# Warm-up matmuls of 256 columns in place of twice as many of 128, and the first Q turned ahead of the first K piece

## The chip, the cores and the metric

The kernel runs on one core of one Trainium2 chip. The metric is the time of one execution on the device in microseconds (us); lower is better. A core has a matrix engine (PE, whose weight loads are listed as PEld), a vector engine (DVE), an activation engine (ACT), GpSimd (POOL) and a sync engine (SP) that here issues most DMAs. Each engine takes its instructions strictly in the order in which they were put down for it; between engines they wait on semaphores.

## The reference, cut to what matters

Attention whose queries are averaged in pairs, followed by a max-out MLP. Batch 8, 8 heads, sequence 1152, head size 64; after the pairing there are 576 queries a head.

```
q_pool = q.reshape(B, H, S // 2, 2, D).mean(axis=3)
scores = 1/sqrt(D) * q_pool @ k^T
attn   = softmax(scores)
x      = (attn @ v), heads side by side       # 4608 x 512
g      = maximum(x @ w1, x @ w2)              # 4608 x 1024
out    = g @ w_out                            # 4608 x 512, float32
```

All inputs are float32; the kernel works in bfloat16 with float32 accumulation. The ones that the changed matmuls multiply are no part of this: their products are never read.

## The kernel before, in words

Two heads form a pair; there are 32 pairs. For each pair K, Q and V are loaded, cast to bfloat16 (Q: its two rows added, which is the pairing), and K and Q are transposed so that the head size lies on the partitions. Scores come in groups of 512 columns for both heads (`scores`, L302, four or more matmuls into two PSUM banks); one ACT instruction a group takes the exponential (`exps`, L317, a tile of 128x1024). Later matmuls multiply by V (L621, L636), DVE normalizes, and the MLP's matmuls (L760, L803, L846) are woven between.

The order of everything is written out by hand in one long string. Each character is a step: `S` the scores of the next group on PE, `E` its exponential on ACT, `K` and `Q` the transposes of the next piece of K and of Q on PE, `g` and `b` the copies of their results from PSUM to SBUF on DVE, `f` a cast of K on ACT, `k` a cast of K on POOL, `y` the add of Q's rows on DVE, `l` and `u` the next load on SP and on ACT, `F` a fill job. A character puts one step at the end of its own engine's queue, so the string fixes only the order within each engine; steps of different engines are ordered by their data. A second string, `BANKS`, gives the PSUM bank of each PE step in the order of opening.

The first pair comes in pieces so that work can start early. K arrives in four pieces (tiles 0-2, 2-4, 4-6, 6-9); the first two are cast on ACT (L418), the last two on POOL (L424). Each is transposed by PE (`ktrans_pe` with `halves`, L552) and copied to kT by DVE (L568). Q arrives in two pieces (units 0-4 and 4-9, L358 loads); DVE adds the rows (L428, `cast_q0`), PE transposes (`qtrans`, L533), DVE copies to qpT (L540). The first scores need the first piece of both.

Ahead of this PE multiplies ones with ones ("fill"). DVE writes ones into 128 columns of the tile `rem` (L399); PE runs 28 matmuls of 128x128 on them into bank 7 and two fill jobs of two matmuls each (L515); 14 more fill jobs (28 matmuls) stand singly in the string among the first groups of scores. In all there are 60 such matmuls, each with its weight load.

The start of the order string before is `luFFlulllfyKQklgfbSkKEFlgFKSgESyFFlKEFgQSbE`. On PE it reads: fills, K piece 0, Q piece 0, scores 0, K piece 1, F, F, K piece 2, scores 1, scores 2, F, F, K piece 3, F, Q piece 1, scores 3. On DVE: ones, add Q piece 0, copy K piece 0, copy Q piece 0, copy K pieces 1 and 2, add Q piece 1, copy K piece 3, copy Q piece 1.

## Time and profile before

| what | us |
|---|---|
| median of 3 runs | 358.02 |
| lowest and highest of them | 357.6 and 358.13 |
| span of the profiled execution, first to last instruction | 356.4 |
| PE busy | 346.0 (97%) |
| ACT busy | 313.8 (88%) |
| DVE busy | 230.1 (65%) |
| POOL busy | 151.4 (42%) |

The profiled execution's own time is its span; the run's time also holds what lies around the first and the last instruction. In the profile a line such as `L515` is the line of the kernel that recorded the instruction. A group's busy time counts the stretch in which at least one of its instructions is in flight. PE's matmuls overlap, so the durations of single matmuls are longer than the distance from one start to the next. The chain lists the work that ended last, followed back from the end; what is not on it was finished early enough.

### The profile page before, as it was taken

Reading aid. Unit: us, or ns where it says so; the run is one execution under the profiler, and the core shown is the slowest. Engines: PE = TensorE matmul, PEld = TensorE weight load, DVE = VectorE, ACT = ScalarE, POOL = GpSimd, SP = SyncE. Lnnn points to the kernel's source line nnn. Section 1 sums busy time; section 2 is a strip of 40 time slices with the busy share of each in tenths; the row PEclk is TensorE's granted clock in tenths of the full one; section 3 lists DMA queues with packets and bytes.
Section 4 is the critical chain, followed back from the end, with each engine's and each line's share of the span. In section 5 each row is a group of like instructions: output and inputs, shape, how many; then the busy total and the mean of one; then the engine's idle time right before and its main releaser. Section 6 shows DMA issues by size and latency. Waiting matters only on the chain.

```text
span 356.4 us, 13757 instructions
## 1 busy us (share of the span) xinstructions
PE 346.0 (97%) x6178; PEld 218.5 (61%) x6178; DVE 230.1 (65%) x472; ACT 313.8 (88%) x354; POOL 151.4 (42%) x136
## 2 busy tenths in 40 slices
PE   7889999999899999999999999999999999999996
PEld 5556665656564675656666576556576757448753
DVE  2587589974966867985887677785586875414001
ACT  5999999999999899999999989989999796992431
POOL 2625997554564264355544455227444621010000
PEclk9999999999999999999999999999999999999999
DMA  8999999999989989998999699998999943012215
GB/s 271 403 397 398 370 255 309 280 289 261 293 252 279 315 196 350 237 301 183 278 320 260 153 230 301 237 314 234 224 299 255 267 68 75 17 32 47 61 31 148
DMA packets 76699, 84.55 MB, mean 237 GB/s; under 512 B 48480, under 2 KB 49760, under 8 KB 76640
## 3 DMA queue, kind: packets, MB, share of 16 engines
q1 hardware_dynamic: 75856, 83.15, 87.5%
q8 instruction: 48, 0.79, 0.9%
q10 hardware_dynamic: 784, 0.52, 0.5%
q14 instruction: 11, 0.09, 0.1%
HBM read 62.91 MB, written 9.44 MB: 203 GB/s over the span
## 4 chain that ended last, share of the span: by engine, by line
PE 87%; ACT 9%; DMA 2%; issue 1%; SPq 0%; DVE 0%
PE ps L803 25%; PE ps L621 20%; PE ps L302 19%; PE ps L760 16%; ACT et L317 9%; PE ps L636 3%; PE ps L593 2%; DMA qraw<-in_q_dram 2%; PE ps L846 1%; PE ps L552 0%; PE ps L533 0%; SPq L346 0%; DVE qp L428 0%; SPq L358 0%; PE ps L730 0%
## 5 line engine op out<-in xcount | busy, mean ns | idle before, releaser
L317 ACT ACTIVATE et<-ps 128x1024 bf16<-128x1024 f32 (+1 forms) x336 | 302.4, 1019 | 14.5 <-PE ps L302 9.7
L302 PE MATMUL ps<-qpT,kT 64*128 64x256 bf16 (+7 forms) x1162 | 117.3, 283 | 2.7 <-issue 1.1
L485 DVE STREAM_TRANSPOSE qpT<-qp 32x288 bf16<-32x288 bf16 x216 | 101.4, 469 | 10.4 <-PE ps L302 6.1
L760 PE MATMUL ps<-xT,wd 64*128 64x512 bf16 (+3 forms) x832 | 81.2, 311 | 0.2
L302 PEld LDWEIGHTS ps<-qpT,kT 64*128 64x128 bf16 x1162 | 48.3, 94 | 49.7 <-ACT et L317 11.3
L803 PE MATMUL ps<-wo,stage 64*128 64x512 bf16 x544 | 76.4, 376 | 0.0
L435 POOL TENSOR_TENSOR qp<-qraw 128x576 bf16<-128x576 f32 x30 | 42.1, 1406 | 61.1 <-DMA qraw<-in_q_dram 57.3
L621 PEld LDWEIGHTS ps<-vE,et 128*128 128x128 bf16 x1728 | 54.9, 97 | 13.9 <-ACT et L317 9.3
L621 PE MATMUL ps<-vE,et 128*128 128x65 bf16 x1728 | 60.7, 193 | 0.7 <-issue 0.3
L771 DVE TENSOR_SCALAR stage<-ps 128x1024 bf16<-128x1024 f32 (+3 forms) x41 | 39.7, 970 | 21.1 <-PE ps L760 20.6
L760 PEld LDWEIGHTS ps<-xT,wd 64*128 64x128 bf16 x832 | 35.6, 94 | 22.2 <-PE ps L760 1.9
L405 POOL TENSOR_SCALAR kbf<-kraw 128x1152 bf16<-128x1152 f32 x31 | 35.7, 1153 | 26.3 <-DMA kraw<-in_k_dram 25.6
L803 PE MATMUL ps<-w,xT 64*128 64x512 bf16 x272 | 40.8, 377 | 0.0
L803 PEld LDWEIGHTS ps<-wo,stage 64*128 64x128 bf16 x544 | 26.4, 94 | 20.5
L445 POOL TENSOR_SCALAR vE<-vraw 128x1152 bf16<-128x1152 f32 x24 | 27.4, 1154 | 19.4 <-PE ps L636 10.8
L809 DVE COPY stage<-ps 128x1024 f32<-128x1024 f32 x14 | 17.1, 1224 | 23.1 <-PE ps L803 23.0
L468 POOL TENSOR_SCALAR stage<-et 128x1152 bf16<-128x1152 bf16 x14 | 16.1, 1152 | 35.5 <-ACT et L317 35.5
L654 DVE TENSOR_TENSOR xnat<-ps,rc 128x256 bf16<-128x256 f32 (+2 forms) x71 | 27.6, 397 | 2.0
L651 DVE RECIPROCAL rc<-ps 128x4 f32<-128x4 f32 (+2 forms) x64 | 11.6, 182 | 25.9 <-PE ps L621 25.5
L621 PEld LDWEIGHTS ps<-stage,et 128*128 128x128 bf16 x576 | 18.1, 97 | 2.7 <-issue 2.6
L621 PE MATMUL ps<-stage,et 128*128 128x65 bf16 x576 | 19.7, 193 | 0.0
L803 PEld LDWEIGHTS ps<-w,xT 64*128 64x128 bf16 x272 | 12.5, 94 | 8.8 <-DVE stage L771 0.2
(55 smaller groups left out, 155.4 us busy)
## 6 DMA issues: line engine op xcount, KB each, us to landing
vraw<-in_v_dram SPq DMA_DIRECT2D x32, 576.0 KB, 6.1
kraw<-in_k_dram SPq DMA_DIRECT2D x31, 576.0 KB, 6.7
qraw<-in_q_dram SPq DMA_DIRECT2D x31, 576.0 KB, 6.3
out_dram<-stage SPq DMA_DIRECT2D x24, 256.0 KB, 4.1
out_dram<-stage SPq DMA_DIRECT2D x21, 128.0 KB, 3.4
xT<-in_moe_w_dram SPq DMA_DIRECT2D x4, 512.0 KB, 12.2
stage<-in_moe_w_out_dram SPq DMA_DIRECT2D x4, 512.0 KB, 14.1
stage<-in_moe_w_dram SPq DMA_DIRECT2D x4, 512.0 KB, 13.2
```

What stands on the lines that cost most here:

```text
L302: last = e.matmul(ps[:, h, col:col + hi - lo], kT[i % 3][rows(h), t, :], qpT[i % 3][rows(h), lo:hi], start=True, stop=True)
L317: op("ACT", lambda e: e.activation(et2[:, :, c:c + z - a], ps[:, :, a - g * W:z - g * W], EXP, scale=scale), r=[f"b{m}", f"b{m + 1}"], w=w ...
L405: op("POOL", lambda g: g.tensor_scalar(kbf[s][:, :, :, :].rearrange("p t h d -> p h t d"), kraw[r][:, :, :, :], 1.0, 1.0, ALU.mult, ALU.mu ...
L435: op("POOL", lambda g: g.tensor_tensor(qpf[s][:, :, :], qraw[r][:, :, 0, :], qraw[r][:, :, 1, :], ALU.add), r=[f"qraw{r}"], w=[f"qp{s}.0", ...
L445: return g.tensor_scalar(vE[r][:, :, :, 0:D].rearrange("p t h d -> p h t d"), vraw[s][:, :, :, :], 1.0, 1.0, ALU.mult, ALU.mult)
L485: op("DVE", lambda e: e.transpose(view[dst:dst + 32, :, 32 * pb:32 * pb + 32], qpf[s][src:src + 32, :, 32 * db:32 * db + 32]), r=[f"qp{s}. ...
L621: last = e.matmul(fb[m][:, at * 66:at * 66 + 65], et[:, a:a + P], vE[vs][:, t, half, 0:65], start=(t == 0), stop=(t == NT - 1))
L654: todo.append(evac_op("DVE", lambda e, m, z=z, at=at, num=num, dst=dst: e.tensor_tensor(dst, a(m)[z, at:at + num, 0:D], rc[k][z, at:at + n ...
L760: last = e.matmul(fb[m + k][:, 0:size], wd[z, ct, (f0 + k) * P:(f0 + k + 1) * P], xT[z, ct, n0:n1], start=(turn == 0 and ct == 0), stop=(t ...
L771: return e.tensor_scalar_max(gT[:, f0:f0 + 2, g0:g0 + size], wide[m // 2][:, :, 0:size], 0.0)
L803: last = e.matmul(fb[m + k][:, :], lhs, rhs, start=(turn == 0 and j == 0), stop=(turn == 1 and j == NC_ + NF - 1))
L809: return e.tensor_copy(osb2[:, o:o + 2, :], wide[m // 2][:, :, :])
```

## The change

The ones cover 256 columns instead of 128, and each fill matmul multiplies 128 of them by all 256; 14 instead of 28 stand at the start, and one instead of two in each fill job. The total of columns streamed by fills stays as it is; the matmuls on ones fall from 60 to 30, with as many weight loads. In the order string `KQ` becomes `QK` and the copy `b` goes ahead of the copy `g`, so on PE the first Q piece is transposed ahead of the first K piece and on DVE it is copied first. The bank string is turned to match, so each step keeps its bank. Costs named in the code (`cost=`) are not used by it.

```
-    FILL = 28
+    FILL = 14
...
-        "0124605424023623462032424660232342630240624702402064202420472042646264246024604640164604264126402406"
+        "0142605424023623462032424660232342630240624702402064202420472042646264246024604640164604264126402406"
...
-                op("DVE", lambda e: e.memset(rem[:, 0, :, :], 1.0), w=["rem0"], cost=0.1)
-                op("PE", lambda e: fill(e, 7, FILL), r=["rem0"], w=["b7"], cost=0.0563 * FILL, mode="f",
+                op("DVE", lambda e: e.memset(rem[:, 0:2, :, :], 1.0), w=["rem0"], cost=0.15)
+                op("PE", lambda e: fill(e, 7, FILL), r=["rem0"], w=["b7"], cost=0.1126 * FILL, mode="f",
...
-            one = rem[:, 0, :, :].rearrange("p h c -> p (h c)")
+            one = rem[:, 0:2, :, :].rearrange("p t h c -> p (t h c)")
             for _ in range(n):
-                last = e.matmul(fb[m][:, 0:P], one, one, start=True, stop=True)
+                last = e.matmul(fb[m][:, 0:2 * P], one[:, 0:P], one, start=True, stop=True)
             return last
...
-            return Job(("f", n), 1, [(["rem0"], 0.0563 * 2, "f", False, lambda e, m: fill(e, m, 2))], [])
+            return Job(("f", n), 1, [(["rem0"], 0.1126, "f", False, lambda e, m: fill(e, m, 1))], [])
...
-            "luFFlulllfyKQklgfbSkKEFlgFKSgESyFFlKEFgQSbESlFkSFEFFKlEySFSgESlqFFEFQlSbEFkSQElbKvSEgSlESceAAEATcESA"
+            "luFFlulllfyQKklbfgSkKEFlgFKSgESyFFlKEFgQSbESlFkSFEFFKlEySFSgESlqFFEFQlSbEFkSQElbKvSEgSlESceAAEATcESA"
```

## The prediction

> **What bounds the kernel now.** I read the page's totals first, then the chain in order of time, because the change lies wholly in the first 14 us and only the chain tells what an early microsecond is worth.

> ```profile
> span 356.4 us, 13757 instructions
> ...
> PE 346.0 (97%) x6178; PEld 218.5 (61%) x6178; DVE 230.1 (65%) x472; ACT 313.8 (88%) x354; POOL 151.4 (42%) x136
> ```

> PE is the busy engine over the whole span, but the start looks different. The chain, first rows:

> ```profile
> 2.24 5.91 DMA qraw<-in_q_dram
> 8.15 0.02 issue
> 8.17 0.50 DVE qp L428
> 8.67 0.04 issue
> 8.72 0.34 PE ps L533 x10
> 9.06 0.34 PE ps L302 x4
> 9.40 0.02 issue
> 9.43 15.70 ACT et L317 x17
> 25.12 0.04 issue
> 25.17 0.41 PE ps L552 x16
> ```

> Until 8.15 us the end of the kernel hangs on one transfer, the second piece of the first Q. From it a short line of single steps (add, transposes, scores) leads to the fourth exponential at 9.43, and from there 17 exponentials follow without a gap until 25.12. Only then does PE take the chain. So whatever the change does ahead of 9.43 counts only if it moves that transfer, that line of steps, or the feeding of ACT between 9.43 and 25.12.

> The start in single steps, from the timeline, all engines together in order of time:

> ```profile
> 0.90 0.17 DVE L399 MEMSET rem<- 128x128 bf16 x1 [0.90 <-PEq L1027]
> ...
> 1.12 3.41 PE L515 MATMUL ps<-rem 128*128 128x128 bf16 x32 [1.12 <-DVE rem L399]
> ...
> 3.92 0.43 DVE L428 TENSOR_TENSOR qp<-qraw 128x256 bf16<-128x256 f32 x1 [2.85 <-DMA qraw<-in_q_dram]
> ...
> 4.31 0.86 ACT L418 ACTIVATE kbf<-kraw 128x256 bf16<-128x256 f32 x2 [1.20 <-DMA kraw<-in_k_dram]
> ...
> 4.78 0.23 PE L552 MATMUL ps<-ident,kbf 64*128 64x64 bf16 x4 [0.25 <-ACT kbf L418]
> ...
> 4.95 0.31 PE L533 MATMUL ps<-ident,qp 64*64 64x64 bf16 x8
> 5.06 0.29 DVE L568 COPY kT<-ps 128x256 bf16<-128x256 bf16 x1 [0.71 <-PE ps L552]
> 5.22 1.03 POOL L424 TENSOR_SCALAR kbf<-kraw 128x256 bf16<-128x256 f32 x2 [3.65 <-DMA kraw<-in_k_dram]
> 5.30 0.29 DVE L540 COPY qpT<-ps 128x256 bf16<-128x256 bf16 x1
> ...
> 5.65 0.39 PE L302 MATMUL ps<-qpT,kT 64*128 64x256 bf16 x4 [0.39 <-DVE qpT L540]
> ```

> The first Q piece is ready at 3.92 + 0.43 = 4.35, the first K piece at 4.31 + 0.86/2 = 4.74, and PE is done with the fills at about the time the Q is ready. As K stands first, Q waits 0.6 us for it (4.95 instead of 4.35), and the first scores wait for the copy of Q, the last of the four steps.

> ACT in this stretch:

> ```profile
> 6.08 2.85 ACT L317 ACTIVATE et<-ps 128x1024 bf16<-128x1024 f32 x3 [0.91 <-PE ps L552]
> 9.43 2.85 ACT L317 ACTIVATE et<-ps 128x1024 bf16<-128x1024 f32 x3 [0.49 <-PE ps L302]
> ```

> Three exponentials end at 8.93, then ACT idles 0.49 us for the line of steps that the transfer holds. This idle is the cover of everything that is gained or lost ahead of it.

> **The change part by part.** *Q ahead of K.* A hand-over from DVE to PE takes 0.06 (the copy of Q ends at 5.59, scores start at 5.65), from PE to DVE 0.04 to 0.05 (transposes end at 5.01, copy at 5.06). Q's 8 transposes then start at 4.35 + 0.06 = 4.41 and end at 4.72; their copy runs from 4.77 to 5.06. K's start stays at 4.78, bound by the cast, since Q's instructions have long been issued; its copy starts at 5.06 as before, ends at 5.35, and the scores start at 5.41 instead of 5.65: 0.24 us earlier. What follows on PE and DVE moves with it: K piece 1 has been cast by 4.31 + 0.86 = 5.17, piece 2 by 5.22 + 1.03/2 = 5.74, before they are asked for. So the three exponentials run from 5.84 to 8.69. The fourth does not move: its scores stand behind the second Q's transposes on PE, and the copy of K piece 3 stands behind the second Q's add on DVE, and both wait for the landing at 8.15. What is late next is thus that transfer, and the idle time of 0.49 becomes 0.73. Gain on the end: 0. Its bounds are 0 and, if that transfer were free by then, -0.24.

> The moved step brings 8 transposes on PE and one copy on DVE, no DMA. On PE it passes K's four transposes, on DVE K's copy; SP, ACT and POOL keep their queues word for word, so no transfer is issued earlier or later. It adds one thing: PE now waits for Q's add ahead of K's cast. Behind that wait stand K, the scores and all later PE work. In this trace Q is ready 0.39 us before K; Q would have to come later than that to hold K back, and the scores need both anyhow.

> *Ones of 256 columns.* The memset takes 0.17 for 128 columns. The wider one is not in the trace; the nearest rows are DVE's copies of several widths and its widest slow form:

> ```profile
> L568 DVE COPY kT<-ps 128x256 bf16<-128x256 bf16 x3 | 0.9, 292 | 1.5 <-PE ps L552 1.5
> L540 DVE COPY qpT<-ps 128x576 bf16<-128x576 bf16 x4 | 1.8, 458 | 2.8 <-PE ps L533 2.8
> L498 DVE TENSOR_REDUCE wo<-stage 128x1024 bf16<-128x1024 f32 x4 | 4.8, 1210 | 0.0
> ```

> The copies give (458 - 292)/320 = 0.52 ns a column, 0.07 us for 128 more; the slow form 1.2 ns, 0.15 us; nothing at all is the other end. I take 0.07, as a memset is nearer to a copy. Fills start at 1.19.

> *Half as many fills.* Their pace shows the clock better than the clock column does:

> ```profile
> 3.00:3.50 0.50, 0.50 (x8) 0.50 (x6) 0.00 (x0) 0.11 (x1) 0.00 (x0) 1.00 1.05 325
> ```

> ```profile
> 1.73 2.80 PE L515 MATMUL ps<-rem 128*128 128x128 bf16 x26
> ```

> ```profile
> 3.97 0.56 PE L515 MATMUL ps<-rem 128*128 128x128 bf16 x5
> ```

> ```profile
> 10.36 0.51 PE L515 MATMUL ps<-rem 128*128 128x128 bf16 x6
> ...
> 11.51 0.29 PE L515 MATMUL ps<-rem 128*128 128x128 bf16 x2
> ```

> From 1.73 to 3.97 there are 26 - 5 = 21 steps in 2.24 us, 0.107 each; late fills step (0.51 - 0.29)/4 = 0.055. So PE runs at half speed up to about 4.2 us, although the window prints a clock of 1.00 (it has no record for that time), and at full speed after. A fill of 128 columns is paced by its columns in both states, with its weight load beside it, so one of 256 should cost what two cost now: 0.213 slow, 0.11 fast. The 16 at the start then end as before to within the memset's 0.07, about 4.42 instead of 4.37, which is when Q comes ready: no cost. The 14 single jobs stream the same columns; each drops one weight load that was hidden anyway. They all lie between 6.03 and 13.9, where the chain is a transfer, the line of steps (no fill in it), or ACT: 0 on the end. If the cover were gone, 14 times the difference between two small and one large would count, by these rows under 0.01 us each, 0.1 in all.

> [...]

> *Sum:* 0 on the span of 356.4 (bounds -0.24 and +0.1). The runs' median lies 358.02 - 356.4 = 1.6 above the span, around which nothing changes. Forecast 358.0 us.

> **The rivals.**
> *The clock opens later or closes again (slower).* The fills are there in effect to hold the clock. It opened 4.2 - 1.12 = 3.1 us after the first fill. If what opens it counts instructions or weight loads rather than columns, half as many may not do it, and PE is at half speed when the line at 8.72 runs; that is the point from which it decides. Price: the line's ten transposes stream 5 pairs of 64 columns and its scores 2 pairs of 256, at 128 columns in 0.053 about 0.13 + 0.21 = 0.34 us, which doubles: +0.34. Then, per exponential of 0.95 us (2.85/3), PE's scores alone grow from 0.21 to 0.43, and with fills (0.11 a job) and 18 transposes of 64 columns in pairs (0.24) the load goes from some 0.6 to 1.2, over the 0.95 that ACT takes: 0.2 to 0.3 lost at each of three exponentials. Together about +1.0, 359.0. Against it: a fill leaves PE as busy with 256 columns as with two times 128, and in the trace the clock held through the gap from 8.1 to 8.7.

> [...]

> *PE's instruction stream is lighter (faster).* The source view of the fill line has a row for time in which PE stood before a fill for no shown reason:

> ```profile
>   issue: 0.8, 4
> ```

> Four times 0.2 us. If PE's own queue handling is what these are, 30 fewer matmuls and weight loads give back up to 0.8 us, and if ACT between 9.43 and 25.12 is in truth fed late by PE, the end moves by as much: 357.2. Against it: the chain shows no gap in ACT there, so I see no way for it to reach the end. [...]

> *It does not bring Q forward.* If the fills ran over (the memset at +0.15 and the opening late), Q would start up to 0.3 later and the first scores stay at 5.65. The fourth exponential would still be at 9.43: 358.0, no difference.

> **How the numbers follow.** A measurement of this kernel can tell about 0.2% from no change, 0.7 us. Forecast (0 on the end) 0.44; Q not brought forward, also no change, 0.08; clock 0.28; lighter stream 0.20. So faster 0.20, same 0.52, slower 0.28. The clock has more than the lighter stream because it has a path to the end, and the other needs one that the chain doesn't show. The no-change cases alone would span 357.6 to 358.3 (the runs' spread and the bounds). The range must leave out no more than 2 in 10: it takes in 357.2 and 359.0 with 0.3 around them, 356.9 to 359.3.

> **What would show it.** Right: fills in 16 steps of 0.213 to about 4.2, then 0.11; Q's transposes ahead of K's at 4.4; first scores near 5.4; three exponentials ending near 8.7; the idle before the fourth grown to about 0.7; the fourth at 9.4 and 17 without a gap. Wrong: matmuls after 4.5 us still at half pace (clock rival); the second Q's add not at 8.2; gaps in ACT between 9.4 and 25; or a difference that first appears after 25 us, where the change touches nothing.

## The result: slower, and the profile after

The changed kernel takes 361.33 us (median of 22 runs, 358.57 to 366.32), the kernel before 358.43 in the same 22 rounds (357.02 to 360.69). The ratio is 1.0067, with a 95% interval of 1.0046 to 1.0088: 0.67% or 2.4 us slower. The ratio leaves out the two of the 22 runs that lie more than 1.5% above the fastest (364.89 and 366.32), so it is a little below that of the medians, which differ by 2.9 us. The forecast was no change, 358.0, in a range that ended at 359.3. The profiled execution has a span of 361.8 us against 356.4: it loses 5.4 us, more than the medians differ.

The start did what it should. Rows of the changed kernel's timeline, PE and DVE in the first 9 us, then ACT:

```profile
0.93 0.27 DVE L399 MEMSET rem<- 128x256 bf16 x1 [0.93 <-PEq L1027]
...
1.26 3.33 PE L515 MATMUL ps<-rem 128*128 128x256 bf16 x16 [1.26 <-DVE rem L399]
...
4.52 0.31 PE L533 MATMUL ps<-ident,qp 64*64 64x64 bf16 x8
...
4.76 0.23 PE L552 MATMUL ps<-ident,kbf 64*128 64x64 bf16 x4
...
5.42 0.39 PE L302 MATMUL ps<-qpT,kT 64*128 64x256 bf16 x4 [0.42 <-DVE kT L568]
...
7.27 0.49 DVE L428 TENSOR_TENSOR qp<-qraw 128x320 bf16<-128x320 f32 x1 [0.58 <-DMA qraw<-in_q_dram]
```

```profile
5.85 19.42 ACT L317 ACTIVATE et<-ps 128x1024 bf16<-128x1024 f32 x22 [0.68 <-PE ps L552]
25.46 4.69 ACT L317 ACTIVATE et<-ps 128x1024 bf16<-128x1024 f32 x5 [0.19 <-PE ps L302]
```

Q goes ahead of K, the first scores start at 5.42, and the clock opens at 4.18 by the trace's clock record (4.20 before). In this execution the second Q piece also came in early enough (its add starts at 7.27 instead of 8.17), so 22 exponentials run with no gap from 5.85: the fourth is 0.85 us earlier than before.

The time is lost later. I paired the exponentials of the two traces by their number and took the lag of the changed kernel, that is, how much later each starts than before: -0.85 us at the fourth, +0.17 at 31 us, +0.8 at 131, +1.3 at 182, and then one jump from +1.3 to +4.4 at 285 us and to +5.3 at 292. The waits of PE between 100 and 300 us, in the view of who waited for whom, first before, then after (us in total, times, longest):

```profile
PEld ps L621 <- issue: 2.8, 13, 0.2
```

```profile
PEld ps L621 <- issue: 6.4, 17, 2.5
PE ps L621 <- issue: 2.9, 2, 2.4
```

"Issue" is idle time for which the profile knows no releaser. Before, it comes in portions of 0.2 us ahead of the weight loads; after, matmuls multiplying by V stand still for 2.4 us at a stretch. The place on PE's timeline, first before, then after:

```profile
281.95 2.35 PE L621 MATMUL ps<-stage,et 128*128 128x65 bf16 x72
```

```profile
283.23 1.93 PE L621 MATMUL ps<-stage,et 128*128 128x65 bf16 x58
287.54 0.93 PE L621 MATMUL ps<-stage,et 128*128 128x65 bf16 x14 [2.38 <-issue]
```

The same 72 matmuls, without any wait written between them, run through before, and after they are cut into 58 and 14. And the stall costs more than itself. The windows view of the changed kernel around it (columns: busy time of PE, PEld, DVE, ACT, POOL, then granted clock, DMA share and GB/s):

```profile
285.00:287.50 2.50, 0.16 (x6) 0.06 (x3) 0.76 (x2) 0.06 (x1) 2.50 (x3) 1.00 1.10 99
287.50:289.00 1.50, 1.46 (x20) 1.09 (x21) 0.46 (x3) 0.00 (x0) 0.55 (x1) 0.50 0.88 344
289.00:291.00 2.00, 2.00 (x18) 0.92 (x14) 0.52 (x2) 1.94 (x2) 1.15 (x1) 0.53 0.31 68
```

After the idle time the clock is at half from 287.48 to 290.90 by the clock record, 3.41 us. The lag grows by 4.1 us in all (from +1.3 to +5.4): 2.4 are the stall, and the other 1.7 are half of the 3.41 us at half clock. In three of the 22 runs the mean clock is 0.995 as here; they are the three slowest, 363.5 to 366.3. The other 19 have a median of 360.82, still 2.4 us above 358.43, so the halved clock makes single runs worse but the loss does not need it.

What PE lacked there, as the rest of this document argues, were instructions. The page of the profile lists a DMA queue that carries them:

```profile
q8 instruction: 48, 0.79, 1.0%
```

48 packets with 0.79 MB are blocks of 16 KB. PE has 6148 matmuls, as many weight loads and some 60 waits, about 12,400 instructions; 0.79 MB over these is 64 bytes each, and by that estimate a block holds 256 of them, 128 pairs of weight load and matmul less the waits. I counted the matmuls in both traces up to each stall without a releaser, and set the time at which a block's transfer ended beside the time at which PE went on. A stall is given from the start of the matmul ahead of it to the start of the one behind it, so it is some 0.2 to 0.35 us longer than the idle time:

| kernel | stall on PE, us | matmul it stands before | block transfer, us | from its end to PE, us |
|---|---|---|---|---|
| before | 28.49 to 29.04 | 474 | 26.54 to 27.64 | 1.40 |
| before | 91.22 to 92.70 | 1620 | 90.30 to 91.40 | 1.30 |
| after | 28.89 to 30.12 | 474 | 27.57 to 28.70 | 1.42 |
| after | 130.03 to 130.76 | 2258 | 127.90 to 129.24 | 1.52 |
| after | 284.96 to 287.54 | 5062 | 285.14 to 286.20 | 1.34 |

The matmuls 1620, 2258 and 5062 are 9, 14 and 36 times 127.4 behind 474, though these are different steps of the program in the two kernels: the stalls lie at block borders, and each ends 1.3 to 1.5 us after a transfer. The eleven traces of the experiments below bear this out: over all thirteen there are 28 idle stretches of 0.3 us or more on PE without a releaser, and every one stands before matmul 474 or 1, 9, 10, 14, 36 or 37 blocks of 127.4 behind it. That a block is asked for when PE begins the one ahead of it is my reading, as no trace records the asking. Counted from there, up to 4.7 us pass until its transfer starts (before and after), about 2 us in the median from 95 to 290 us (2.1 before, 2.3 after); behind 290 us, where the page of the changed kernel has 19 to 62 GB/s on the DMA queues up to 353 us (101 to 403 ahead of that), it is 1.1 us at most. So a block of short matmuls was used up before the next one had come. In the place above the block ahead of the border holds some 63 matmuls at 17 ns and 58 at 32 ns in the changed kernel, and PE needs 3.4 us for it; the next block's transfer started 3.6 us after PE had begun it. Before, a border lies in the same run of 72, after 28 of them; the block ahead of it holds fewer short matmuls and takes 4.3 us, the transfer started after 0.8 us, and PE does not stall. The change takes 30 pairs out of the start, and with that moves all later borders by 30 matmuls.

That gives a reckoning that can be tested. For each block I took the time that PE needs for it at the pace of before, and the shortage against a need of delay + 1.1 (transfer) + 1.4 us, averaged over the delays seen in the two traces. This is an estimate, made after the result was known. Summed: 3.2 us with the borders of before, 5.6 with 30 pairs fewer, 4.6 with 16 fewer, 4.3 with 64 more, 5.6 with 98 more (98 is 128 - 30), 3.2 again with 128 more.

### The profile page after: what moved, and what is told of

The parts are those of the page before. It is cut to its first block, busy times and chain, and to the rows that moved or that the text cites. A ratio compares the mean times of both kernels' runs of the same rounds, so it can differ in the third digit from the quotient of the medians.

```text
span 361.8 us, 13697 instructions
## 1 busy us (share of the span) xinstructions
PE 348.6 (96%) x6148; PEld 217.6 (60%) x6148; DVE 230.3 (64%) x472; ACT 314.1 (87%) x354; POOL 151.3 (42%) x136
## 4 chain that ended last, share of the span: by engine, by line
PE 75%; ACT 15%; DMA 6%; issue 2%; DVE 1%; POOL 0%; SPq 0%
PE ps L803 21%; PE ps L621 17%; PE ps L302 16%; ACT et L317 15%; PE ps L760 14%; DMA xT<-in_moe_w_dram 4%; PE ps L636 2%; DMA qraw<-in_q_dram 2%; PE ps L593 2%; PE ps L846 1%; PE ps L515 1%; POOL qp L435 0%; PE ps L552 0%; DVE xT L498 0%; DVE stage L809 0%
## 5 line engine op out<-in xcount | busy, mean ns | idle before, releaser
L317 ACT ACTIVATE et<-ps 128x1024 bf16<-128x1024 f32 (+1 forms) x336 | 302.6, 1021 | 19.5 <-PE ps L302 14.5
L302 PE MATMUL ps<-qpT,kT 64*128 64x256 bf16 (+7 forms) x1162 | 118.0, 284 | 2.6 <-DVE kT L568 0.7
L760 PE MATMUL ps<-xT,wd 64*128 64x512 bf16 (+3 forms) x832 | 82.1, 314 | 0.2
L302 PEld LDWEIGHTS ps<-qpT,kT 64*128 64x128 bf16 x1162 | 48.3, 94 | 50.5 <-ACT et L317 11.3
L803 PE MATMUL ps<-wo,stage 64*128 64x512 bf16 x544 | 76.4, 376 | 0.0
L405 POOL TENSOR_SCALAR kbf<-kraw 128x1152 bf16<-128x1152 f32 x31 | 35.6, 1151 | 22.4 <-DMA kraw<-in_k_dram 20.6
L803 PE MATMUL ps<-w,xT 64*128 64x512 bf16 x272 | 40.8, 377 | 0.0
L803 PEld LDWEIGHTS ps<-wo,stage 64*128 64x128 bf16 x544 | 26.4, 94 | 20.5
L803 PEld LDWEIGHTS ps<-w,xT 64*128 64x128 bf16 x272 | 12.5, 94 | 8.9 <-DVE stage L771 0.2
```

The lines of the kernel that those rows point to most:

```text
L302: last = e.matmul(ps[:, h, col:col + hi - lo], kT[i % 3][rows(h), t, :], qpT[i % 3][rows(h), lo:hi], start=True, stop=True)
L317: op("ACT", lambda e: e.activation(et2[:, :, c:c + z - a], ps[:, :, a - g * W:z - g * W], EXP, scale=scale), r=[f"b{m}", f"b{m + 1}"], w=w ...
L405: op("POOL", lambda g: g.tensor_scalar(kbf[s][:, :, :, :].rearrange("p t h d -> p h t d"), kraw[r][:, :, :, :], 1.0, 1.0, ALU.mult, ALU.mu ...
L760: last = e.matmul(fb[m + k][:, 0:size], wd[z, ct, (f0 + k) * P:(f0 + k + 1) * P], xT[z, ct, n0:n1], start=(turn == 0 and ct == 0), stop=(t ...
L803: last = e.matmul(fb[m + k][:, :], lhs, rhs, start=(turn == 0 and j == 0), stop=(turn == 1 and j == NC_ + NF - 1))
```

## Experiments

All ratios are to the kernel before, run in the same rounds, with 95% intervals. Theory 1 is the one above; theory 2 says that the earlier start shifts the later transfers.

**The two halves apart.** Fills alone (the changed kernel with order and banks of before; cut):

```
-            "luFFlulllfyQKklbfgSk...    BANKS "0142605424...
+            "luFFlulllfyKQklgfbSk...    BANKS "0124605424...
```

> The 256-column fills alone; K stays ahead of Q. Theory 1 (instruction supply): PE's instructions arrive in blocks of 16 KB, 48 of them in the trace; the stalls without a releaser in both traces lie at matmuls 474, 1620, 2258 and 5062, which are 9, 22 and 27 times 127.4 apart from the first, and each ends 1.3 to 1.5 us after a 16 KB instruction transfer ended. 30 matmuls and their weight loads fewer move the block borders by 30 matmuls, into the dense runs of attention-times-V matmuls, where a block is used up in 3.4 us instead of 4.4 to 4.8. Worked out from the pace of the trace before and the delays of the instruction transfers in both traces: 5.6 us of such stalls in a run instead of 3.2, so +2.3 us here, ratio about 1.0065, the whole change. Theory 2 (earlier start): the first scores come 0.24 us earlier and all later transfers fall otherwise; then this kernel, whose first scores come no earlier, is like the one before, ratio 1.000.

The expectation miscounts the distances: they are 9, 14 and 36 blocks from the first. Measured: 362.18 us (6 runs), 1.0106 (1.0066 to 1.0145). Q first alone, the opposite edit (fills of before, order and banks of the change):

> Q ahead of K alone; 60 fills of 128 columns as before. Theory 1: the count of PE's instructions is that of before and so are the block borders; ratio 1.000 to 0.999 (the first scores 0.24 us earlier). Theory 2: the whole change, ratio about 1.0065.

Measured: 358.03 us, 1.000 (0.9978 to 1.0021). The fills alone make the whole loss, Q first neither costs nor gains: theory 2 is out, since here the first scores start earlier without a loss, and the fills alone lose without them (5.79). PE's timeline of the fills-alone kernel shows the cut at the same place, 14 matmuls from the end:

```profile
283.81 1.67 PE L621 MATMUL ps<-stage,et 128*128 128x65 bf16 x50
286.05 0.58 PE L621 MATMUL ps<-stage,et 128*128 128x65 bf16 x14 [0.56 <-issue]
```

(The view begins at 284 us; the run of matmuls began at 283.56 and has 58.) Here PE is idle for only 0.56 us: the block's transfer started 1.7 us after it was asked for, against 3.6 in the changed kernel.

**The count restored.**

```
-                op("PE", lambda e: fill(e, 7, FILL), ...      # 14 of 256 columns
+                op("PE", lambda e: pad(e, 7, 44), ...         # 44 of 81 columns
```

> The changed kernel with its first 14 fills cut into 44 of 81 columns: 60 matmuls on ones as before, Q first, all later fills with 256 columns. Theory 1: 30 more matmuls than the changed kernel, and faster by 2.3 us for it: ratio to before 1.000. Theory 2 and a third one, that the 256 columns themselves cost (the clock, the memset): like the changed kernel, about 1.0065.

Measured: 358.72 us, 1.0005 (0.9984 to 1.0025). More matmuls, and the loss is gone, with the wide ones, the memset and the order of Q as in the change. In its timeline the 72 matmuls are whole again:

```profile
282.94 2.43 PE L627 MATMUL ps<-stage,et 128*128 128x65 bf16 x72
```

This execution also bears on the clock rival. Its clock opened only at 13.32 us, ACT had to wait for scores, and the fourth exponential started at 10.43, 1.0 us later than before; at the end the lag is 1.1 us, close to the price that the prediction put on a late clock. But this is the kernel without the loss, and in the changed kernel's trace, which loses 5.4 us, the clock opened at 4.18.

**Half the dose.**

```
-                op("DVE", lambda e: e.memset(rem[:, 0, :, :], 1.0), ...
+                op("DVE", lambda e: e.memset(rem[:, 0:2, :, :], 1.0), ...
...
-            [(["rem0"], 0.0563 * 2, "f", False, lambda e, m: fill(e, m, 2))]
+            [(["rem0"], 0.1126, "f", False, lambda e, m: wide_fill(e, m, 1))]   # 1 of 256; first 28 of 128 kept
```

> Before, with only the 16 fill jobs made of one matmul of 256 columns; the 28 first fills have 128. 16 matmuls and weight loads fewer. Theory 1 by the same reckoning: 4.6 us of stalls instead of 3.2, +1.4 us, ratio 1.004, between before and the change. Theory 2: 1.000.

Measured: 359.58 us, 1.0031 (1.0014 to 1.0049). The place of the cut moves with the count:

```profile
283.81 1.34 PE L627 MATMUL ps<-stage,et 128*128 128x65 bf16 x39
286.57 1.00 PE L627 MATMUL ps<-stage,et 128*128 128x65 bf16 x28 [1.42 <-issue]
```

(Of the 44 matmuls ahead of the cut the view, which begins at 284 us, holds 39.) The cut stands 28 matmuls from the end instead of 14: with 16 pairs fewer the border falls 14 matmuls earlier in the program than with 30 fewer.

**Adding late.** Two kernels add work on PE well behind the start of the changed kernel, ahead of the first matmul of L803 in the program, which then overwrites it:

```
+                    if n == 0 and j == 0 and turn == 0:
+                        for _ in range(30):
+                            e.matmul(fb[m][0:32, 0:16], ident[:, 0:32], ident[:, 0:16], start=True, stop=True)
```

> The changed kernel with 30 small matmuls (32x16, with their weight loads) added on PE ahead of the first p job, at about matmul 1890, near 113 us; their products are overwritten. Theory 1 (instruction supply): from there on the block borders are those of before again, and the blocks at matmuls 2131, 3533 and 4934 stall some 2.5 us less in sum by the reckoning (1.4 each instead of 0.5, 0.4 and 0.7); the added work costs 30 times about 0.03, 0.8 to 0.9 us. So added work makes it faster than the changed kernel by about 1.6 us: ratio to before about 1.002. Rival (the loss is made in the first 14 us, by the clock or the early transfers, and added work only costs): 1.009.

```
+                        for _ in range(4):
+                            e.matmul(fb[m][:, :], ident[:, :], w21[:, 0, :], start=True, stop=True)
```

> The changed kernel with 4 matmuls of 512 columns at the same place instead: about the same PE time (4 times 0.216, 0.86 us), but only 4 instead of 30 more instructions of each kind. Theory 1: the borders move by 4 and the stalls stay, so it is slower than the changed kernel by what it adds: ratio to before about 1.009. Rival: like the 30 small ones, whatever they give.

Both expectations place the added work wrongly: in the traces it runs at 69.4 to 70.3 us (30 small, from matmul 1178 on) and from 68.4 us (4 wide), not near 113. The argument is the same with that place, but it puts the border at 1620 behind the added work too.

Measured: 30 small 359.92 us, 1.0047 (1.0019 to 1.0075); 4 wide 361.32 us, 1.0082 (1.0050 to 1.0115). By the medians the 30 small ones are 1.4 us faster than the 4 wide ones, where 2.5 were expected, and 30 more matmuls do not make the changed kernel slower; the intervals overlap, so the times alone would not settle it. The waits of PE from 100 to 300 us do, first with 30 small, then with 4 wide:

```profile
PEld ps L621 <- issue: 3.1, 14, 0.3
```

```profile
PEld ps L621 <- issue: 4.6, 16, 0.8
PE ps L621 <- issue: 1.3, 2, 0.7
```

With the borders moved back at 70 us the long stalls from 100 us on are gone; with four wide matmuls they stay. The border at 1620 leaves PE idle for 1.04 us with the small ones, as before (1.12), and not in the changed kernel: there too the borders are those of before. The lag against the trace before says the same: with the small ones it is +2.6 us at 71 us and +2.65 at the end, with the wide ones +1.5 at 70 us and +3.5 at the end. What remains with the small ones was thus lost early, after a lead of 0.8 at the fourth exponential: 1.95 us by a wait for V and the half clock that followed it in this execution (17.55 to 20.96), 0.5 at the border of 474, and 1.0 for the added work itself.

**What delays a block.** Loads of pairs 8 to 31 cut to 16 of 128 partitions, in the changed kernel and in the one before:

```
-                kraw[s][:, :, lo:hi, :] ...  k[...][:, :, lo * D:hi * D]
+                kraw[s][0:16 if i >= 8 else P, :, lo:hi, :] ...  k[...][0:16 if i >= 8 else P, :, lo * D:hi * D]
```

and the same for Q and V; the results of these pairs are then not the reference's. DMA transposes and output stores stay whole.

> The changed kernel, but from pair 8 on each load of K, Q and V moves 16 instead of 128 partitions (the rest keeps old data). Theory 1 with its cause of the delay: an instruction block is asked for at a border and waits behind the bulk loads; without them it starts within about 1 us, as the trace before shows after 290 us, where loads have ended, and no block border stalls after pair 8 (from about 75 us). Then this kernel is equal to the next one within 0.2%, both being below 1.000 of before by what stalls and late loads cost, some 1 to 3 us. If the delay does not come from the loads, it stays slower than the next one by about 2 us.

> The kernel before with the same light loads from pair 8 on (16 of 128 partitions, the rest old data). Theory 1: equal to the changed kernel with light loads within 0.2%. If the delay of instruction blocks does not come from the loads: faster than that one by about 2 us, as without the edit.

Measured: 358.93 us, 1.0009 (0.9987 to 1.0031) and 357.85 us, 0.9980 (0.9959 to 1.0001). The changed kernel loses most of its handicap, 2.4 us to 1.1, but the two are not within 0.2% of each other as I expected, and their intervals overlap. The delay from border to transfer, median of the blocks from 95 to 290 us, goes from about 2 us (before and after) to 0.4 and 0.6 (the same two with light loads); the largest from 4.6 (after) to 2.1. The waits from 100 to 300 us of the changed kernel with light loads:

```profile
PEld ps L621 <- issue: 3.0, 14, 0.2
```

No long stall is left there. Cutting the loads thus takes most of the delay away. It does not show that a block waits for loads alone. Ahead of the longest stall of the changed kernel the block was asked for at 281.6 and its transfer started at 285.14, and no load was issued in that time; the DMA work issued ahead of it was stores and transposes:

```profile
277.71 2.23 SPq L835 DMA_DIRECT2D out_dram<-stage  x3
280.05 1.29 SPq L475 DMA_TRANSPOSE kT<-kbf  x1
281.38 2.20 SPq L703 DMA_TRANSPOSE xT<-xnat  x1
285.84 0.38 SPq L370 DMA_DIRECT2D vraw<-in_v_dram  x1
```

Of the 16 DMA engines' time in these 3.6 us, packets under 512 bytes take 75%, packets of 2048 bytes (the size of an output row) 39%, and packets of 2304 bytes (K and V) 3%; records of packets overlap, so the sum exceeds 100%. With light loads the same block starts 0.9 us after it is asked for, though small packets fill that time too. How loads, transposes and stores share the delay was not tried apart. The two light kernels still differ by 1.1 us in the medians. In their traces the lag between them is 1.4 us by 33 us already, ahead of pair 8, where the loads are whole (the border of 474 stalls 1.05 us in the one and not in the other), and 1.6 at the end. That part was not tried by itself.

**Whole blocks.** The kernel before with its first 28 fills cut into more and smaller ones of about the same columns in all:

```
-                op("PE", lambda e: fill(e, 7, FILL), ...
+                op("PE", lambda e: pad(e, 7, 92, 39), ...     # or 126 of 28, or 156 of 23 columns, 32-column weights
```

> The kernel before (K first), its 28 first fills cut into 92 of 39 columns with 32-column weights: 64 matmuls and weight loads more than before, streamed columns as before. Theory 1 with a period of one block (128 pairs of weight load and matmul, 16 KB): the borders move by 64, 4.3 us of stalls by the reckoning instead of 3.2: ratio 1.003. Rival (the number of instructions as such, fewer is slower): 1.000 or below.

> The same with 126 first fills of 28 columns: 98 more than before, which modulo a block of 128 is the same as the 30 fewer of the change. Theory 1: the stalls of the changed kernel, 5.6 us instead of 3.2: ratio 1.0065, although nothing but small fills in the start has been added. Rival: 1.000 or below.

> The same with 156 first fills of 23 columns: 128 more, one whole block. Theory 1: the borders are where they were in the kernel before: ratio 1.000 to 1.001, faster than with 98 more by over 2 us. Rival (added fills cost by their number, through the start): slower than with 98 more.

Measured: 64 more 359.95 us, 1.0038 (1.0005 to 1.0070); 98 more 361.92 us, 1.0078 (1.0042 to 1.0113); 128 more 360.89 us, 1.0039 (1.0004 to 1.0074). 98 more pairs do what 30 fewer do, and the timeline shows the same cut as the change itself, 58 and 14:

```profile
284.00 1.93 PE L627 MATMUL ps<-stage,et 128*128 128x65 bf16 x58
288.94 0.93 PE L627 MATMUL ps<-stage,et 128*128 128x65 bf16 x14 [3.01 <-issue]
```

It too was followed by 3.41 us at half clock. 128 more are faster again than 98 by 1.0 us in the medians, which speaks against the number as such, though the intervals overlap; and they do not come back to 1.000: a part of the expectation failed. The 156 fills take 4.34 us, where the 28 first fills and the two jobs behind them took 3.41 before, and the first exponential starts at 7.20 instead of 6.08, but by 32 us the lag in that trace is down to 0.1. Its lag grows by 1.8 us between 142 and 146 us, where the chain shows a late V load (8.35 us to land) and DVE, not a block border, and by 0.8 at 288 us, where the border of matmul 5190 stalls (0.66 us idle). Whether the remaining 0.4% is such waits or the start stays open.

Measured against the reckoning, in us over before (ratio less 1, times 358.4). The row of the change is no test, as its trace went into the reckoning:

| pairs | kernel | expected | measured |
|---|---|---|---|
| 0 | Q first alone | 0 | 0.0 |
| 0 | count restored | 0 | 0.2 |
| -16 | jobs only | 1.4 | 1.1 |
| -30 | the change | 2.3 | 2.4 |
| -30 | fills alone | 2.3 | 3.8 |
| +64 | 92 small fills | 1.1 | 1.4 |
| +98 | 126 small fills | 2.3 | 2.8 |
| +128 | 156 small fills | 0 | 1.4 |

The order fits but for 128 more; the sizes miss by up to 1.5 us (fills alone, six runs with an interval of 2.4 to 5.2 us; 128 more). By the reckoning no count would be clearly faster than before: its lowest stretch, 0 to 20 more pairs, lies within 0.2 us of the kernel before, and none of these counts was run.

## Why the prediction was wrong

- *Q ahead of K:* right in size, and right about the first scores (forecast 5.41, measured 5.42; 5.59 when done alone). The gain on the end was forecast as 0 and measured as 1.000 (0.9978 to 1.0021) when done alone. The reason given for the 0 did not hold, so that part is luck: it was that the second Q piece lands at 8.15 and the fourth exponential stays at 9.43. That was one execution. In the thirteen traces the add of this piece starts between 6.79 and 8.17 us, and the fourth exponential moved: 8.58 in the changed kernel, 8.75 with Q first alone. In the changed kernel the gain was used up by 31 us, by the wait for a transfer of MLP weights (landed 20.6) and the stall at matmul 474; with Q first alone it was still 0.78 us at 92 us and gone at 131.
- *Memset:* forecast +0.07, measured 0.27 instead of 0.17. Covered, as said.
- *Fills:* their pace was right, 0.213 us slow and 0.11 fast; a wide one lasts as long as two small ones.
- *The step that failed* is the one that set 30 fewer matmuls and weight loads at "0 on the end" because their PE time was hidden. PE time was not their price. Their number decides where PE's instruction stream is cut into blocks, for the whole program, and I looked for their effect only where they stand. The runs showed in its place 2.4 us (1.0067) for 30 pairs fewer, 1.1 for 16 fewer, and 0.2 (1.0005) with the count restored. The page of the profile showed the instruction queue (q8, 48 packets), and a stall of 1.47 us at a border was in the trace before; I read neither.
- *The rival that came out on the right side* (the clock, +1.0, 0.28) had the wrong mechanism: the clock opened on time, the half clock at 287.48 followed the stall, and the 19 runs without any half clock lose as much. No run leaves the fills out, so what they do for the clock was not shown. A late or closed clock did cost time: the late opening with the count restored cost 1.1 us, and in the execution with 30 small matmuls the clock closed again at 17.55 us, and with the wait ahead of it that cost 1.95 us. But that is not what the change costs. The other rival had the right object, PE's instruction stream, and the wrong sign. The four waits of 0.2 us that I quoted for it are still there with half the fills (`issue: 0.8, 4` in both).
- The prediction named "a difference that first appears after 25 us, where the change touches nothing" as the sign of its failure, and that is what came.

## What to carry to other kernels

In this long unrolled program 30 matmuls and weight loads fewer in the first 14 us moved every later block border of PE by 30 matmuls, and at the end of a block full of matmuls at 17 and 32 ns PE ran dry for 2.4 us. (Other engines were not tried.) Look in the profile for idle time put down to "issue" inside a run of equal matmuls, and compare it with the instruction queue's transfers. Before believing that an edit of a few instructions helps or hurts, run it once more with the count restored by harmless ones.
